# Fifty no-ops in ScalarE's stream, ahead of the skip products of the third tile

## The chip, the cores and the metric

The kernel runs on one core of one Trainium2 chip. The experiments came in three sets, each on another chip of this kind. The metric is the device time of one execution in microseconds (us). Before the change it was 213.41 us (median of 3 runs, 212.93 to 216.17). TensorE, VectorE, ScalarE, GpSimd and SyncE are called PE, DVE, ACT, POOL and SP in the profile; PEld is PE's weight load.

## The reference

It mixes a state-space branch and a dense branch over 2048 rows of width 640. Cut to what matters:

```python
def reference(A_x, ..., gate_w):
    x = A_x                                            # [1, 2048, 640]
    g = sigmoid((x * gate_w).sum(-1, keepdims=True))
    a = ssm(x)                                         # scan over the rows; ends in
                                                       #   y = 2*real(h @ C.T) + x * Dskip
    b = gelu(x @ w1 + b1) @ w2 + b2                    # 640 -> 1728 -> 640
    return g * a + (1 - g) * b
```

`x * Dskip` is the skip product of the title.

## The kernel before

The 2048 rows are four tiles of 512. The kernel lists its operations with their dependencies and assumed durations; a small scheduler in it fixes each engine's order, and waits are inserted for the dependencies. PE results go through eight PSUM banks, handed out in turn. One tile's output is made as follows (cuts marked with `...`):

```python
def outsT(q, mid=None):
    pieces = [(4, 0, HT), (4, HT, 512)] + [(d, 0, 512) for d in range(4)]
    mb = [next_bank() for _ in pieces]          # six banks for the second dense layer
    ...                                         # PE: mt_{q}, ScalarE evicts it to E1T (6 pieces)
            op(f"e1t_{q}_{d}_{t0}", "act", ..., [("bank", bank), ...], [("E1T", d, t0)], f_ev, prio=5)
    ...
    for d in range(KD):                         # KD = 5: the skip products, in place in xT

        def f_dx(d=d):
            return inc("act", nc.scalar.activation(xT[q][:, d, :], xT[q][:, d, :], ACT.Copy, scale=cols2[:, 1, d:d + 1]))

        op(f"dx_{q}_{d}", "act", d_act(512), [("cols2", 1)], XK0[d] if q == 0 else [("xT", q, d)], f_dx, prio=20)

    for d in range(KD):                         # five C-projection groups of ten matmuls
        bank = next_bank()                      # the third of them gets mb[0] again
        ...                                     # PE: ct_{q}_{d}; ScalarE evicts it to E2T
    ...
    op(f"s{q}", "dve", ..., K2, XT[q], lambda: tt(xf, xf, e2, ALU.add), prio=P)   # first reader of the products
```

The order on ScalarE is not that of the text. The third tile's products (q = 2) can run as soon as that tile's first-layer matmuls have read xT, so the scheduler puts them between that tile's Gelus and the E1T evictions of the second tile (q = 1).

Of the kernel before, what the change touches and what calls it, by code (L numbers as in the profile page):

```python
# [147 lines left out]
class Prog:  # L148
# [8 lines left out]
    def op(self, name, eng, dur, reads, writes, fn, prio=None, lat=0.0, after=()):  # L157
        deps = {}
        for k in reads:
            for w in self.last_w.get(k, ()):  # L160
                deps[w.idx] = w
        for k in writes:
            for w in self.last_w.get(k, ()):
                deps[w.idx] = w
            for r in self.last_r.get(k, ()):
                deps[r.idx] = r
        for a in after:
            deps[a.idx] = a
        deps = list(deps.values())
        E = self.E  # L170

        def run(eg, deps=deps, eng=eng, fn=fn):
            E.wait(eng, *[d.done for d in deps if not (eng == "pe" and d.eng == "pe")])
            return fn()

        it = self.sch.add(name, eng, dur, deps, run, prio=prio, lat=lat)
        for k in writes:
            self.last_w[k] = [it]
            self.last_r[k] = []
        for k in reads:  # L180
            self.last_r.setdefault(k, []).append(it)
        return it


def bass_gated_mix__ssm_conv_s5__dense_activation_gelu__prompt_kernel(
# [18 lines left out]
    _, S, D = A_x.shape  # L204
# [5 lines left out]
    NQ = S // 512  # L210
# [15 lines left out]
    with ExitStack() as es:  # L226
# [83 lines left out]
        def inc(eng, ins):  # L310
            return E.inc(eng, ins, eng + "_s")
# [8 lines left out]
        def d_act(n):  # L320
            return 0.26 + n * 0.00084
# [590 lines left out]
        def outsT(q, mid=None):  # L912
# [39 lines left out]
            for d in range(KD):  # L952

                def f_dx(d=d):
                    return inc("act", nc.scalar.activation(xT[q][:, d, :], xT[q][:, d, :], ACT.Copy, scale=cols2[:, 1, d:d + 1]))

                op(f"dx_{q}_{d}", "act", d_act(512), [("cols2", 1)], XK0[d] if q == 0 else [("xT", q, d)], f_dx, prio=20)
# [125 lines left out]
```

## Time and profile before

| | before |
|---|---|
| time, median (range) | 213.41 us (212.93 to 216.17) |
| profiled execution | 213.5 us, clock 1.00 |
| span of its instructions | 212.2 us |
| ScalarE idle between the third tile's products and the next eviction | 10.97 us |

The page of the profile, kernel before: busy time by engine with the share of the span, then the engines' shares of the chain of work that ended last.

```profile
PE 208.4 (98%) x1102; PEld 104.4 (49%) x1102; DVE 190.1 (90%) x240; ACT 103.2 (49%) x177; POOL 4.2 (2%) x12
...
PE 94%; SPq 2%; DMA 2%; issue 0%; DVE 0%
```

PE is the bound, and ScalarE is not in the chain at all. Next the ScalarE timeline around the third tile's products. The columns are start, duration, engine and line, operation, output <- input, count, and in brackets the idle time before with what ended it.

```profile
106.76 0.69 ACT L660 ACTIVATE Gl<-ps,cols 128x512 bf16<-128x512 f32 x1 [0.39 <-PE ps L653]
107.84 0.69 ACT L660 ACTIVATE Gl<-ps,cols 128x512 bf16<-128x512 f32 x1 [0.39 <-PE ps L653]
108.43 3.16 ACT L955 ACTIVATE xT<-xT,cols 128x512 bf16<-128x512 bf16 x5
122.56 3.15 ACT L938 ACTIVATE E1T<-ps,cols 128x256 bf16<-128x256 f32 x6 [10.97 <-PE ps L931]
```

The five products (L955) follow the last Gelu (L660) directly. Then ScalarE idles for 10.97 us until PE gives it something to evict. The PE timeline of the same stretch, kernel before:

```profile
107.64 14.22 PE L920 MATMUL ps<-Gl,W2sb 128*128 128x256 bf16 x78
121.80 0.71 PE L931 MATMUL ps<-Gt,W2sb 64*128 64x512 bf16 x6
122.44 10.96 PE L967 MATMUL ps<-Hb,CT 128*128 128x512 bf16 x50
```

There is no idle time in brackets: PE goes straight on. L967 is the C projection, five groups of ten matmuls. Its third group starts two fifths in, at about 122.5 + 2 x 2.16 = 126.8 us, and needs the bank that the first E1T eviction frees.

### The profile page before, as it was taken

The numbers are of one execution on the slowest core, as the hardware profiler recorded it, in microseconds if no ns is written. First come the engines' busy times: TensorE is split into PE (matmuls) and PEld (weight loads), VectorE is DVE, ScalarE is ACT, GpSimd is POOL, SyncE is SP. The second block draws the span as 40 slices with busy tenths as digits, with TensorE's granted clock in tenths as the row PEclk, the third lists the DMA queues.
The fourth block names the chain that finished last, engine by engine and source line by source line (L and its number), as shares of the span: only waits on it lengthen the run. The fifth ranks groups of instructions, "written<-read, shape, count | busy, mean of one in ns | idle before, by whom it ended". The sixth has DMA issues, their size and how long they took to land.

```text
span 212.2 us, 2742 instructions
## 1 busy us (share of the span) xinstructions
PE 208.4 (98%) x1102; PEld 104.4 (49%) x1102; DVE 190.1 (90%) x240; ACT 103.2 (49%) x177; POOL 4.2 (2%) x12
## 2 busy tenths in 40 slices
PE   8999999999999999999999999999999999999995
PEld 4344444444554444444464444444456444567774
DVE  2599999999999998999999999899999999499734
ACT  2579556679850453556680072456660037523320
POOL 1000000300000000000100000000010000000000
PEclk9999999999999999999999999999999999999999
DMA  6999999999300020063274000009440000007341
GB/s 170 279 238 192 176 209 298 277 173 225 76 0 3 5 44 0 0 127 76 48 62 111 3 0 0 0 2 166 95 124 39 0 3 0 0 0 109 87 116 63
DMA packets 48424, 19.08 MB, mean 90 GB/s; under 512 B 41372, under 2 KB 47132, under 8 KB 48412
## 3 DMA queue, kind: packets, MB, share of 16 engines
q1 hardware_dynamic: 46752, 17.59, 40.1%
q0 software_dynamic: 1600, 1.32, 4.3%
q8 instruction: 8, 0.13, 0.3%
q10 hardware_dynamic: 60, 0.01, 0.1%
q14 instruction: 4, 0.03, 0.1%
HBM read 8.41 MB, written 2.63 MB: 52 GB/s over the span
## 4 chain that ended last, share of the span: by engine, by line
PE 94%; SPq 2%; DMA 2%; issue 0%; DVE 0%
PE ps L653 22%; PE ps L696 20%; PE ps L920 20%; PE ps L967 15%; PE ps L783 7%; PE ps L832 5%; DMA W1sb<-in_B_w_dram 2%; PE ps L631 2%; SPq L340 1%; PE ps L674 1%; SPq L333 1%; PE ps L931 1%; PE ps L797 0%; DVE W1sb L866 0%
## 5 line engine op out<-in xcount | busy, mean ns | idle before, releaser
L653 PE MATMUL ps<-xT,W1sb 128*128 128x512 bf16 x220 | 48.1, 379 | 0.0
L736 DVE TENSOR_TENSOR_SCAN W<-atab,V 128x1280 bf16<-128x1280 f32 x16 | 44.3, 2811 | 0.3
L696 PE MATMUL ps<-xT,BT 128*128 128x512 bf16 x200 | 43.8, 379 | 0.0
L920 PE MATMUL ps<-Gl,W2sb 128*128 128x512 bf16 (+1 forms) x234 | 42.7, 344 | 0.0
L660 ACT ACTIVATE Gl<-ps,cols 128x512 bf16<-128x512 f32 x44 | 29.8, 693 | 15.5 <-PE ps L653 15.5
L653 PEld LDWEIGHTS ps<-xT,W1sb 128*128 128x128 bf16 x220 | 21.5, 98 | 26.0
L967 PE MATMUL ps<-Hb,CT 128*128 128x512 bf16 x150 | 32.9, 379 | 0.0
L920 PEld LDWEIGHTS ps<-Gl,W2sb 128*128 128x128 bf16 x234 | 22.9, 98 | 19.3
L705 ACT ACTIVATE U<-ps 128x512 bf16<-128x512 f32 x40 | 23.7, 596 | 15.6 <-PE ps L696 15.6
L696 PEld LDWEIGHTS ps<-xT,BT 128*128 128x128 bf16 x200 | 19.5, 98 | 23.7 <-ACT Gt L682 0.4
L938 ACT ACTIVATE E1T<-ps,cols 128x512 bf16<-128x512 f32 (+1 forms) x18 | 9.4, 624 | 36.0 <-PE ps L931 36.0
L967 PEld LDWEIGHTS ps<-Hb,CT 128*128 128x128 bf16 x150 | 14.5, 98 | 17.9 <-DVE V L488 0.6
L975 ACT ACTIVATE E2T<-ps 128x512 bf16<-128x512 f32 x15 | 9.1, 604 | 13.6 <-PE ps L967 13.6
L783 PE MATMUL ps<-W2sb,Gl 128*128 128x320 bf16 x104 | 14.8, 299 | 0.0
L606 DVE SCALAR_TENSOR_TENSOR trf<-xn,gwb 128x640 bf16<-128x640 bf16 x16 | 13.2, 822 | 0.4
L488 DVE TENSOR_TENSOR V<-V,W 128x1280 bf16<-128x1280 bf16 x16 | 12.5, 821 | 0.3
L488 DVE TENSOR_TENSOR Hb<-Hb,V 128x1280 bf16<-128x1280 bf16 x16 | 12.5, 821 | 0.3
L488 DVE TENSOR_TENSOR V<-mr,U 128x2560 bf16<-128x2560 bf16 x8 | 11.9, 1492 | 0.3
L783 PEld LDWEIGHTS ps<-W2sb,Gl 128*128 128x128 bf16 x104 | 10.1, 98 | 4.3 <-issue 0.3
L488 DVE TENSOR_TENSOR Hb<-c,W 128x2560 bf16<-128x2560 bf16 x8 | 11.9, 1489 | 0.2
L488 DVE TENSOR_TENSOR V<-s,W 128x2560 bf16<-128x2560 bf16 x8 | 11.9, 1484 | 0.0
L488 DVE TENSOR_TENSOR W<-mi,U 128x2560 bf16<-128x2560 bf16 x8 | 11.9, 1483 | 0.0
(91 smaller groups left out, 150.1 us busy)
## 6 DMA issues: line engine op xcount, KB each, us to landing
W2sb<-in_B_w_dram SPq DMA_DIRECT2D x1, 2080.0 KB, 8.6
out_dram<-xn SPq DMA_DIRECT2D x3, 640.0 KB, 4.8
W1sb<-in_B_w_dram SPq DMA_DIRECT2D x5, 256.0 KB, 4.1
xn<-in_A_x_dram POOLq DMA_DIRECT2D x2, 640.0 KB, 7.1
trf<-grow SPq DMA_DIRECT2D x3, 256.0 KB, 5.0
xn<-in_A_x_dram SPq DMA_DIRECT2D x1, 640.0 KB, 7.2
W1sb<-in_B_w_dram SPq DMA_DIRECT2D x1, 480.0 KB, 5.4
out_dram<-W1sb SPq DMA_DIRECT2D x3, 160.0 KB, 1.8
```

The source lines that it names most:

```text
L488: return inc("dve", nc.vector.tensor_tensor(out=o, in0=a, in1=b, op=o_))
L606: t = inc("dve", nc.vector.scalar_tensor_tensor(out=scr[:, :], in0=xn[q % 2][:, c, :], scalar=1.0, in1=gwb[:, :], op0=ALU.mult, op1=ALU.mu ...
L653: t = nc.tensor.matmul(PS[bank][:, :], W1sb[:, k, jf * 128:(jf + 1) * 128], xT[q][:, k, :], start=(k == 0), stop=(k == KD - 1))
L660: return inc("act", nc.scalar.activation(Gl[q % 2][:, jf, :], PS[bank][:, :], ACT.Gelu_apprx_tanh, bias=b1col[:, jf:jf + 1]))
L696: t = nc.tensor.matmul(PS[bank][:, :], BT[:, ci, kd, k * 128:(k + 1) * 128], xT[q][:, kd, :], start=(kd == 0), stop=(kd == KD - 1))
L705: return inc("act", nc.scalar.activation(dst, src, ACT.Copy, scale=1.0 if ci == 0 else -1.0))
L736: t = inc("dve", nc.vector.tensor_tensor_scan(out=g[:, ci, :], data0=a, data1=v[:, ci, :], initial=0.0, op0=ALU.mult, op1=ALU.add))
L783: t = nc.tensor.matmul(PS[bank][:, 0:HALF], Gl[q % 2][:, jf, t4 * 128:(t4 + 1) * 128], W2sb[:, jf, cols], start=False, stop=False, skip_gr ...
L832: t = nc.tensor.matmul(PS[bank][:, 0:n], H[b % NHB][:, ci, k, s * 128:(s + 1) * 128], CT[:, ci, k, cols], start=(i == 0), stop=(i == 2 * K ...
L920: t = nc.tensor.matmul(PS[bank][:, 0:t1 - t0], W2sb[:, jf, d * 128:(d + 1) * 128], Gl[q % 2][:, jf, t0:t1], start=(jf == 0), stop=False)
L938: return inc("act", nc.scalar.activation(E1T[:, d, t0:t1], PS[bank][:, 0:t1 - t0], ACT.Identity, bias=cols2[:, 0, d:d + 1]))
L967: t = nc.tensor.matmul(PS[bank][:, :].rearrange("p (s t) -> p s t", s=2), CT[:, ci, k, d * 128:(d + 1) * 128], Hb[:, 2 * (q % 2):2 * (q % ...
```

## The change

The intent is to see what fifty no-ops cost at a place where ScalarE has nothing to do afterwards. The whole diff:

```diff
@@ -952,6 +952,8 @@
             for d in range(KD):

                 def f_dx(d=d):
+                    for _ in range(10 if q == NQ - 2 else 0):
+                        nc.scalar.nop(nofuse=True)
                     return inc("act", nc.scalar.activation(xT[q][:, d, :], xT[q][:, d, :], ACT.Copy, scale=cols2[:, 1, d:d + 1]))
```

## The prediction

> **What bounds the kernel now.** TensorE. The busy-share table gives PE 208.4 us of a 212.2 us span (98%), VectorE 190.1 us (90%), ScalarE only 103.2 us (49%). The chain of work that ended last is 94% PE and holds no ScalarE instruction. ScalarE can cost time only where PE or VectorE waits for it.
>
> **What the change does.** Ten no-ops before each of the five ScalarE products that scale xT of tile q = 2 by the skip vector: 50 instructions, no data, no semaphore, nothing removed or moved. The durations that the kernel's scheduler uses are untouched: every engine keeps its order.
>
> **Where they fall.** In the ScalarE timeline the third tile's five products run from 108.43 to 111.59 us (about 0.71 us each, starts about 0.61 us apart), right after the tile's last Gelu (107.84 us). They cannot come earlier: they overwrite xT, which the first-layer matmuls read until 107.8 us. After them ScalarE sits idle for 10.97 us, until the matmuls for the next E1T eviction end at 122.5 us.
>
> **Cost of the no-ops.** The trace has no no-op on ScalarE; the closest is a bare semaphore instruction of its sequencer, recorded at 17 ns. [...] My estimate from these is 20 to 60 ns each, 1 to 3 us for 50. [...] ten no-ops (0.2 to 0.6 us) should hide under the product before them (0.61 us), and the first ten under the last Gelus. The products should end between 111.6 and 114.5 us.
>
> **Critical path.** None of it. Three slacks would have to be used up:
> 1. the 10.97 us before the E1T evictions: about 0.22 us per no-op, even if nothing overlaps;
> 2. then another 3.8 us or so: the first E1T eviction (over at 123.0 us) frees the bank that the third C-projection group takes at about 126.8 us;
> 3. the reader of the products, VectorE's first addition into this tile's xT, waits for E2T evictions that start at 176 us: over 60 us later.
>
> The stream grows by 3.2 KB (64 bytes an instruction); the trace shows a few 8 KB instruction reads of 0.4 to 0.7 us each. They may shift; that should not show.
>
> **Prediction.** 213.4 us, the time before. Range 212.6 to 214.8, the scatter of the runs (212.93 to 216.17 before). Faster by over 2%: 0.01. Within 2%: 0.97. Slower by over 2%: 0.02.
>
> **What would show it right or wrong.** The third set of products starts at 108.4 to 109.0 us, its starts 0.6 to 0.75 us apart; the idle time before the second set of E1T evictions shrinks from 10.97 us by 0 to 3 us; that set still starts at about 122.5 us, released by PE; PE's busy time stays about 208.4 us, with no hole between 107 and 134 us; the chain stays 94% PE.
>
> **What would make it wrong.** A no-op that costs over about 0.3 us[...], so that evictions come late and PE waits for banks; a stalled instruction fetch on ScalarE later, where the last tile's evictions have only about 1 us of idle each; or runs in a slower state.

The forecast's sum came to 213.4 us, the time before and nothing added: the 1 to 3 us for 50 no-ops were to fall into ScalarE's 10.97 us of idle time.

## The result

| | before | after |
|---|---|---|
| time, median (range) | 213.30 us (212.93 to 216.17, 4 runs) | 212.86 us (212.52 to 213.04, 4 runs) |
| span of the profiled execution | 212.2 us | 211.7 us |
| semaphore instructions on ScalarE | 6 | 7 |
| no-op records on ScalarE | 0 | 0 |

The ratio of after to before is 0.998 (95% interval 0.9961 to 0.9999). Ratios here are the mean time of one kernel's fast runs over the mean of the other's fast runs of the same rounds, so not quite the ratio of the medians beside them. All four runs of after and its profiled run are fast, at clock 1.00. Before's fourth run came with this result; its 216.17 us is just over 1.5% above its fastest run and so counts as slow, and its three fast runs have a median of 213.18 us.

The page of the profile, kernel after, busy time and chain. (A few matmul records are missing from this trace: 1088 of 1102.)

```profile
PE 208.0 (98%) x1088; PEld 104.8 (50%) x1102; DVE 190.2 (90%) x240; ACT 103.2 (49%) x177; POOL 4.2 (2%) x12
...
PE 97%; DMA 1%; issue 0%; DVE 0%
```

The ScalarE timeline, kernel after:

```profile
107.97 0.69 ACT L660 ACTIVATE Gl<-ps,cols 128x512 bf16<-128x512 f32 x1 [0.39 <-PE ps L653]
108.56 3.16 ACT L957 ACTIVATE xT<-xT,cols 128x512 bf16<-128x512 bf16 x5
122.68 3.15 ACT L938 ACTIVATE E1T<-ps,cols 128x256 bf16<-128x256 f32 x6 [10.97 <-PE ps L931]
```

The PE timeline, kernel after:

```profile
107.77 14.22 PE L920 MATMUL ps<-Gl,W2sb 128*128 128x256 bf16 x77
121.93 0.71 PE L931 MATMUL ps<-Gt,W2sb 64*128 64x512 bf16 x6
122.57 10.96 PE L969 MATMUL ps<-Hb,CT 128*128 128x512 bf16 x50
```

Everything in the middle is 0.13 us later (a start-up difference) and otherwise the same: 0.59 us from the last Gelu to the first product, five products in 3.16 us, 10.97 us idle. This is too good. Fifty instructions have left no record and moved nothing.

The compiled programs say why. ScalarE's stream has 191 instructions of 64 bytes before and 192 after (12,224 and 12,288 bytes), with not one no-op among them; the streams of the other four engines are the same byte for byte. A version with one plain no-op in place of fifty compiles to exactly the same instructions as the changed kernel. The plain no-ops are dropped on the way to the binary. Their one trace is this: a wait that used to ride on the first product (for the load of xT) became a semaphore instruction of its own, which the trace shows at 107.97 us, 17 ns long. So the prediction was made about fifty instructions, and the chip got one.

That leaves two questions. What would fifty real no-ops have cost? And is the 0.2% by which the changed kernel came out ahead scatter, or something?

For the second, compare the ends of the traces. VectorE's last addition and the issue of the last stores, kernel before:

```profile
209.09 0.91 DVE L866 SCALAR_TENSOR_TENSOR W1sb<-ps,gcol,W1sb 128x256 bf16<-128x256 f32 x2 [0.21 <-PE ps L832]
...
209.60 0.81 SPq L875 DMA_DIRECT2D out_dram<-W1sb  x2
```

The same, kernel after:

```profile
209.22 0.91 DVE L866 SCALAR_TENSOR_TENSOR W1sb<-ps,gcol,W1sb 128x256 bf16<-128x256 f32 x2 [0.21 <-PE ps L832]
...
209.73 0.81 SPq L875 DMA_DIRECT2D out_dram<-W1sb  x2
```

The work ends at 209.09 + 0.91 = 210.00 us before and at 210.13 us after, so after is even a little late. But the span ends 2.18 us later before (212.18) and 1.58 us later after (211.71). The span's end is SP's wait for the last store. "Tail" below is the time from VectorE's last end to the record of that wait: 2.15 us before, 1.56 us after. In the trace's DMA records, one 8 KB read of the instruction queue stands out: before, it comes 0.82 us after VectorE's last end, while the last store is landing; after, it comes 1.40 us ahead of it.

### The profile page after: what moved, and what is told of

Read it like the earlier page. It is cut to its first block, busy times and chain, and to the rows that moved or that the text cites. A ratio compares the mean times of both kernels' runs of the same rounds, so it can differ in the third digit from the quotient of the medians.

```text
span 211.7 us, 2729 instructions
## 1 busy us (share of the span) xinstructions
PE 208.0 (98%) x1088; PEld 104.8 (50%) x1102; DVE 190.2 (90%) x240; ACT 103.2 (49%) x177; POOL 4.2 (2%) x12
## 4 chain that ended last, share of the span: by engine, by line
PE 97%; DMA 1%; issue 0%; DVE 0%
PE ps L653 22%; PE ps L696 20%; PE ps L920 20%; PE ps L969 15%; PE ps L783 7%; PE ps L832 5%; PE ps L631 4%; DMA xn<-in_A_x_dram 1%; PE ps L674 1%; PE ps L931 1%; PE ps L419 1%; PE ps L797 0%; DVE W1sb L866 0%; PE ps L438 0%
## 5 line engine op out<-in xcount | busy, mean ns | idle before, releaser
L653 PE MATMUL ps<-xT,W1sb 128*128 128x512 bf16 x215 | 47.5, 379 | 0.3
L696 PE MATMUL ps<-xT,BT 128*128 128x512 bf16 x196 | 43.1, 379 | 0.3 <-issue 0.2
L783 PE MATMUL ps<-W2sb,Gl 128*128 128x320 bf16 x104 | 14.8, 299 | 0.0
```

Of the source, the lines that this page charges most:

```text
L653: t = nc.tensor.matmul(PS[bank][:, :], W1sb[:, k, jf * 128:(jf + 1) * 128], xT[q][:, k, :], start=(k == 0), stop=(k == KD - 1))
L696: t = nc.tensor.matmul(PS[bank][:, :], BT[:, ci, kd, k * 128:(k + 1) * 128], xT[q][:, kd, :], start=(kd == 0), stop=(kd == KD - 1))
L783: t = nc.tensor.matmul(PS[bank][:, 0:HALF], Gl[q % 2][:, jf, t4 * 128:(t4 + 1) * 128], W2sb[:, jf, cols], start=False, stop=False, skip_gr ...
```

## The experiments

"Kept" no-ops carry a one-letter text, `nc.scalar.nop(hint="n", nofuse=True)`; these stay in the program. No-ops with a cycle count also stay in it (fifty compile to 241 instructions on ScalarE), but the simulation that each kernel must pass first does not know them, so they could not be tried.

### Control, and the changed kernel again

`before_again` is the kernel before, with no edit.

> A control: the kernel before, submitted as if it were a new one. It measures how large a ratio plain scatter gives. If the 0.2% that the changed kernel came out ahead is scatter, this ratio should also stray from 1 by 0.1 to 0.3%, within 0.996 to 1.004. If it stays at 1.000 within 0.0005 while the changed kernel repeats 0.998, the 0.2% is real.

`as_given` is the changed kernel, with no edit.

> The changed kernel again, unchanged. In the compiled program no no-op is left: ScalarE's stream has 192 instructions of 64 bytes against 191 before, the one more being a semaphore instruction of 17 ns in the trace. Theory A (the no-ops were never executed, so nothing changed but one 17 ns instruction off the critical path): ratio 0.997 to 1.003, and again 7 semaphore instructions on ScalarE and no no-op record. Theory B (the no-ops are executed but invisible): same time, so this run alone cannot tell them apart; the kept no-ops of the next run can.

Measured: before_again 213.49 us against 213.47 us, ratio 0.9986 (0.9953 to 1.0019); as_given 212.88 us against the same 213.47 us, ratio 0.9979 (0.9937 to 1.0021). As_given again has 7 semaphore instructions on ScalarE and no no-op record. So plain scatter gives a ratio 0.14% off by itself, and the times alone cannot settle a gain of 0.2%. The tails can be compared: 2.36 us in before_again and 1.55 us in as_given, each like its own kind.

### Fifty no-ops that are really there

```diff
-                        nc.scalar.nop(nofuse=True)
+                        nc.scalar.nop(hint="n", nofuse=True)
```

> The same 50 no-ops, each with a one-letter text, which keeps them in the compiled program (241 plus 1 = 242 ScalarE... counted: 241 instructions, 50 of them no-ops). Theory A (the given no-ops were dropped): here, for the first time, no-op records appear on ScalarE between 107.9 and 114.5 us, 20 to 60 ns each, and the third tile's products get further apart or the group of five ends later by 0 to 3 us; the time stays within 0.5% because 10.97 us of ScalarE idle time follow (212.4 to 214.0 us). Theory B (the given ones were executed but not recorded): no no-op records here either, and the ScalarE timeline equals that of the changed kernel.

(The compiled stream has 241 instructions, 50 of them no-ops.) Measured: 213.07 us against 213.47 us, ratio 0.9968 (0.9937 to 0.9999), no cost. The trace now has 50 no-op records on ScalarE, each 14 ns long and mostly 39 ns after the one before; the first starts at 108.15 us and the last at 110.22 us. That is 2.07 us for 50. Theory A holds: the given ones were not there. ScalarE timeline of named50:

```profile
108.14 0.69 ACT L660 ACTIVATE Gl<-ps,cols 128x512 bf16<-128x512 f32 x1 [0.39 <-PE ps L653]
108.73 3.16 ACT L957 ACTIVATE xT<-xT,cols 128x512 bf16<-128x512 bf16 x5
122.86 3.15 ACT L938 ACTIVATE E1T<-ps,cols 128x256 bf16<-128x256 f32 x6 [10.97 <-PE ps L931]
```

Still 0.59 us from Gelu to product, 3.16 us for the five, 10.97 us idle. The no-ops of a group run while the engine is busy with the instruction before, so they delay not even ScalarE itself. This trace shows it: the last no-op belongs to the fifth product and started at 110.22 us, while the third product (from 109.95 us) was still running.

### How much room there is: real copies in place of no-ops

```diff
+        junk = SB("junk", [128, 512], BF16)
...
-                    for _ in range(10 if q == NQ - 2 else 0):
-                        nc.scalar.nop(nofuse=True)
+                    for i in range(4 if q == NQ - 2 else 0):       # 4, 5 or 6
+                        E.wait("act", inc("act", nc.scalar.activation(junk[:, :], xT[q][:, d, :], ACT.Copy)))
```

> Instead of no-ops, 4 real copies (128x512 into a spare tile) before each of the five products, each waiting for the one before it: I estimate 0.65 to 0.75 us each, so ScalarE is occupied 13 to 15 us longer. My slack sum of the prediction (10.97 us of idle, then about 3.8 us until PE needs the first freed bank, 14.8 us in all): cost 0 to 0.3 us. Rival (only the 10.97 us of ScalarE idle is free, everything above it reaches PE): 2 to 4 us. The result in xT must be right in both.

Measured: 212.98 us against 213.47 us, ratio 0.9968 (0.9931 to 1.0004). The ScalarE timeline of copies20, from the last group of copies to the first evictions:

```profile
121.56 2.60 ACT L957 ACTIVATE junk<-xT 128x512 bf16<-128x512 bf16 x4
124.19 0.72 ACT L958 ACTIVATE xT<-xT,cols 128x512 bf16<-128x512 bf16 x1
124.82 3.13 ACT L939 ACTIVATE E1T<-ps,cols 128x256 bf16<-128x256 f32 x6
```

(Each copy waits for the one before it: both write the same spare tile, a race otherwise.) A copy takes 0.65 us, so 13.1 us were added. The evictions start without any idle time before them, 2.2 us later than PE had them ready, and PE does not notice: its fifty C-projection matmuls run in one piece.

```profile
122.54 10.96 PE L970 MATMUL ps<-Hb,CT 128*128 128x512 bf16 x50
```

The idle time of ScalarE is therefore not the whole of the slack; the free banks add to it. The rival's 2 to 4 us are refuted.

Next come five copies and then six. Six were run first.

> 5 real copies before each product: 25 at 0.653 us, 16.3 us. copies30 cost 6.8 us where the slack sum gave 4.8 to 5.2: PE's wait was 4.92 us as summed, and the granted clock then read 0.50 for about 4 us after it. Theory C (the missing 2 us is the clock, which falls only after a long enough wait): here the first E1T eviction is over at about 128.6 us, PE waits 1.6 to 1.9 us from 126.9 us, the granted clock stays 1.00, and the time is 214.3 to 215.3 us. Rival (every wait for a bank brings a further cost of the same kind, in proportion or fixed): 2.3 us or more, with a clock under 1.00.

Measured: 214.80 us against 213.38 us, ratio 1.0048 (1.0001 to 1.0096), clock 1.00 in all four runs. The PE timeline of copies25:

```profile
122.04 4.49 PE L970 MATMUL ps<-Hb,CT 128*128 128x512 bf16 x20
128.13 6.65 PE L970 MATMUL ps<-Hb,CT 128*128 128x512 bf16 x30 [1.60 <-ACT E1T L939]
```

The wait is exactly where the sum put it, ahead of the third of the five groups, and released by the E1T eviction. It is 1.60 us long, with the clock at 1.00, so theory C holds. (This kernel's profiled execution also has the shorter tail, see below: 1.60 - 0.6 is about 1 us, and the ratio gives 1.0 us; the medians are 1.4 us apart.)

> 6 real copies before each product. copies20 showed 0.653 us a copy, so 19.6 us are added. My slack sum (14.8 us): PE stalls at the third C-projection group of the second tile (needed at about 126.9 us, first E1T eviction done at about 131.9 us), 4.8 to 5.2 us, so 217.4 to 218.4 us. Rival (only ScalarE's idle 10.97 us is free): 8.6 us, about 221.5 us. Second rival (a later stage gives the delay back, because VectorE or ScalarE catches up): less than 3 us.

Measured: 220.29 us against 212.96 us, ratio 1.0321 (1.0285 to 1.0358). The PE timeline of copies30:

```profile
122.51 4.49 PE L970 MATMUL ps<-Hb,CT 128*128 128x512 bf16 x20
131.92 9.11 PE L970 MATMUL ps<-Hb,CT 128*128 128x512 bf16 x30 [4.92 <-ACT E1T L939]
```

PE waits 4.92 us, as summed. But the cost is about 6.8 us (3.21% of 213 us), outside the range that I gave. The difference is in the matmuls after the wait: thirty of them take 9.11 us here and 6.65 us in copies25. The windows of copies30 show why (columns: stretch, length, busy us and instructions of PE, PEld, DVE, ACT, POOL, then the granted clock, DMA share and GB/s):

```profile
122.50:127.00 4.50, 4.50 (x22) 1.88 (x20) 4.43 (x7) 4.31 (x8) 0.00 (x0) 1.00 0.00 0
127.00:131.90 4.90, 0.00 (x1) 0.00 (x0) 4.76 (x9) 4.71 (x9) 0.00 (x0) 0.82 0.00 0
131.90:136.00 4.10, 4.08 (x10) 1.50 (x11) 1.39 (x2) 3.62 (x7) 0.00 (x0) 0.50 0.00 0
136.00:138.00 2.00, 2.00 (x8) 0.79 (x7) 0.24 (x2) 0.69 (x2) 0.00 (x0) 0.77 0.00 0
138.00:141.00 3.00, 3.00 (x16) 1.37 (x14) 0.00 (x0) 0.60 (x1) 0.00 (x0) 1.00 0.08 1
```

The granted clock (third number from the end) fell to half during the wait and stayed there until about 136.9 us (a mean of 0.77 from 136 to 138 us is 0.9 us at half and the rest at full); the trace's clock records have it at half from 130.1 to 136.9 us. The sum is then 4.92 us of wait, 9.11 - 6.65 = 2.46 us of half clock, less 0.6 us for the tail: 6.8 us. That it agrees so closely is partly chance: two of the four runs show a mean clock of 0.984 like the profiled one, the other two 0.992, so about half the loss. In the profiled executions waits of 1.60 us (copies25) and 2.41 us (next run) kept the clock at 1.00 and the one of 4.92 us did not. There the half clock began 3.1 us after PE's last matmul (127.0 to 130.1 us) and lasted for about 5 us of work (131.9 to 136.9 us). These runs do not show how long a wait has to be for it.

### How many no-ops it takes

```diff
-                    for _ in range(10 if q == NQ - 2 else 0):
-                        nc.scalar.nop(nofuse=True)
+                    for _ in range(96 if q == NQ - 2 else 0):
+                        nc.scalar.nop(hint="n", nofuse=True)
```

> 96 kept no-ops before each product, 480 in all. named50 took 2.08 us from the first no-op to the last, 41.6 ns each, so 480 take 20.0 us from 108.1 to 128.1 us; the last product then starts at about 128.1 us, and the first E1T eviction is over at about 129.2 us. Slack model: PE waits 2.0 to 2.8 us from 126.9 us, clock 1.00, time 215.0 to 216.3 us. Rival (a no-op never holds up ScalarE): no wait, 212.5 to 213.7 us. Second rival (the sequencer cannot fetch so many instructions that fast): spacing well over 42 ns at each page of 128 no-ops, and a larger cost.

Measured: 216.48 us against 213.38 us over all four runs, 215.39 us over the three fast ones; ratio 1.0125 (1.0033 to 1.0218). The verdict on the time is unclear at the 2% mark, so the profile decides. The profiled execution took 215.39 us, within the expected 215.0 to 216.3. The no-ops ran from 107.73 to 128.04 us. ScalarE and then PE in named480:

```profile
124.00 0.72 ACT L957 ACTIVATE xT<-xT,cols 128x512 bf16<-128x512 bf16 x1 [3.35 <-issue]
128.09 0.72 ACT L957 ACTIVATE xT<-xT,cols 128x512 bf16<-128x512 bf16 x1 [3.37 <-issue]
128.72 3.13 ACT L938 ACTIVATE E1T<-ps,cols 128x256 bf16<-128x256 f32 x6
```

```profile
122.33 4.49 PE L969 MATMUL ps<-Hb,CT 128*128 128x512 bf16 x20
129.23 6.65 PE L969 MATMUL ps<-Hb,CT 128*128 128x512 bf16 x30 [2.41 <-ACT E1T L938]
```

With 96 no-ops to a product there is far too little to hide under (96 at 39 ns are 3.7 us, a product takes 0.72 us), and ScalarE idles 3.07 to 3.65 us before each of the five products, for "issue" in this view. PE waits 2.41 us at the place of the slack model (2.0 to 2.8 expected). Two of the four runs were longer, 217.57 and 219.35 us (the latter counted as slow); both have a mean granted clock of 0.992 against 1.000 in the other two. The clock fell in them, but a mean of 0.992 over 217 us is only about 1.7 us lost (my estimate), and they are 2.2 and 4.0 us longer than the other two. Those runs have no trace, so why the clock fell and where the rest went stays open.

The second rival was partly right: at four places, 126 or 127 no-ops and one or two products from each other, two successive no-ops are 0.32 to 0.33 us apart where 0.039 us is usual. Together these are 128 instructions of 64 bytes, one 8 KB page. The pauses add 1.1 us in all, within the 20.3 us that the burst took. (A fifth gap, of 0.37 us at 109.9 us, lies at no such distance and is not explained.)

### The other engine: no-ops in PE's stream

```diff
                 def f_mm(d=d, bank=bank):                  # the C-projection groups; from the kernel before
+                    for _ in range(10 if q == 1 else 0):
+                        nc.tensor.nop(hint="n", nofuse=True)
                     t = None
```

> The same 50 kept no-ops in the stream of the engine that bounds the kernel: ten before each of the five C-projection groups of the second tile in TensorE's stream (groups of ten matmuls, 2.16 us each, from 122.5 us). Theory R (TensorE's sequencer too reads far enough ahead of its array): no hole in PE and 212.5 to 213.7 us. Rival (the sequencer of the busy engine has no lead, and each no-op costs what one costs on ScalarE, or the 51 ns that TensorE's semaphore instructions show): 2.0 to 3.0 us more, holes of 0.4 to 0.6 us before each group.

Measured: 213.32 us against 213.38 us, ratio 1.0009 (0.9932 to 1.0085). The interval is wide, so the profile decides. (It caught the longest of the four runs, 216.1 us: all of this stretch is 2.4 us later than in the kernel before.) PE timeline of pe50:

```profile
124.20 0.71 PE L931 MATMUL ps<-Gt,W2sb 64*128 64x512 bf16 x6
124.85 10.96 PE L969 MATMUL ps<-Hb,CT 128*128 128x512 bf16 x50
135.65 1.67 PE L696 MATMUL ps<-xT,BT 128*128 128x512 bf16 x7
```

The five groups take 10.96 us, the same as before, with no hole. The first no-op ran at 121.65 us, 3.2 us ahead of the group it stands before. Within a group the no-ops are mostly 70 to 71 ns apart here, more than on ScalarE. Even in the stream of the engine that bounds the kernel, ten no-ops in a row (about 0.7 us) hide here under the matmuls ahead of them.

### The tail: where the page boundary falls

```diff
# one_early
+                    if q == 0 and d == 0:
+                        nc.scalar.nop(hint="n", nofuse=True)
# named128, named129, named256 (n = 128, 129, 256)
+                    for _ in range(n if q == NQ - 2 and d == 0 else 0):
+                        nc.scalar.nop(hint="n", nofuse=True)
```

> One kept no-op, not in the third tile but before the first product of the first tile (at about 49 us). New theory P (page): what the change really altered is the length of ScalarE's stream, 192 instructions for 191, so that the 8 KB instruction read that came at 210.8 us in the kernel before, 0.8 us after VectorE's last instruction and while the last store was landing, comes before that instruction instead; the tail from VectorE's last end to the end of the span falls from 2.15 to 1.56 us. P expects here: the read before VectorE's last end (about 1.4 us before it), a tail of 1.50 to 1.65 us, ratio 0.9965 to 0.9990. Rival S (scatter, or something about the place in the third tile): a tail of 2.1 to 2.4 us as in both profiles of the kernel before, ratio 0.999 to 1.001.

> 128 kept no-ops, all before the third tile's first product. 128 instructions of 64 bytes are exactly 8 KB, one page, so theory P expects the boundary to fall again where it fell in the kernel before: an instruction read 0.5 to 1.3 us after VectorE's last end, a tail of 2.0 to 2.4 us, ratio 0.999 to 1.001. Rival S: as all the other changed kernels, tail 1.5 to 1.65 us. Both expect the no-ops themselves (128 at 39 ns, 5.0 us) to cost PE nothing.

> One no-op more than the run before. Theory P: the read is again ahead of VectorE's last end (1.2 to 1.6 us before it), a tail of 1.50 to 1.65 us, 0.4 to 0.8 us faster in the median than named128. Rival S: equal to named128 within 0.2 us.

> 256 kept no-ops before the third tile's first product, two whole pages of 128. Theory P: as in the kernel before and in named128, an instruction read after VectorE's last end (0.5 to 1.3 us) and a tail of 2.0 to 2.4 us. Rival (named128 was chance): a tail of 1.50 to 1.65 us. PE does not wait in either (256 at 41.6 ns are 10.7 us, under the 14.8 us of slack).

What the traces of all kernels show, by the number of instructions that ScalarE's stream has over the 191 of the kernel before. The read is the last 8 KB instruction read that moves with the length of ScalarE's stream (so I take it for ScalarE's; the 16 KB instruction reads, eight in before and eight in after, are on another queue), in us from VectorE's last end (negative: ahead of it).

| kernel | instructions more | the read | tail, us |
|---|---|---|---|
| before | 0 | +0.82 | 2.15 |
| before_again | 0 | +1.20 | 2.36 |
| pe50 (change on PE only) | 0 | +1.18 | 2.34 |
| named128 | 128 | +0.83 | 2.06 |
| named256 | 256 | +0.84 | 2.00 |
| after | 1 | -1.40 | 1.56 |
| as_given | 1 | -1.50 | 1.55 |
| one_early | 1 | -1.56 | 1.55 |
| named129 | 129 | -1.56 | 1.56 |
| copies20, 25, 30 | 20, 25, 30 | over 31 ahead | 1.55 to 1.56 |
| named50 | 50 | over 79 ahead | 1.56 |
| named480 | 480 | over 84 ahead | 1.55 |

Theory P's tails came true in all four runs made to test it, and no kernel breaks the pattern. A stream longer by a whole number of pages has the read in the tail and loses 0.45 to 0.8 us there; one instruction more, at whatever place, and it does not. The sharpest pair is 128 against 129.

The pattern holds in each of the three sets of runs, so the chip is not the reason: before_again against as_given, named128 against named129, pe50 and named256 against copies25.

The times are much less clear than the tails, because starts differ by over 2 us from run to run (as_given's profiled run reached the third tile's products 2.2 us late, having waited for its first loads). One_early came out at 213.31 us against 212.96 us, ratio 0.9995 (0.9971 to 1.0020); named128 is 213.53 us, ratio 1.0030 (0.9988 to 1.0071). Both miss the ranges that I gave P. Named129 is 213.12 us, ratio 1.0009 (0.9970 to 1.0048); named256 is 213.24 us, ratio 0.9977 (0.9908 to 1.0046). Named129 is 0.41 us faster than named128 in the median, the lower edge of what P expected, with ranges that overlap.

Put together by set, the fast runs of the kernels in which PE does not wait say this. In the first set the median is 213.48 us with the read in the tail (before and before_again, 17 runs) and 212.98 us without (as_given, named50, copies20; 16 runs). In the second set it is 213.16 us with (before and named128, 17 runs) and 213.26 us without (one_early, named129; 12 runs). The third set has no such kernel without the read. (Before was not profiled again in the second and third sets; I place it by its stream.) The gain of the first set did not come back in the second. So the shorter tail is shown in the profiled executions, and a gain in the median is not shown: the 0.2% by which the changed kernel came out ahead stays open.

That the read causes the later landing is shown by moving it by one instruction (named128 and named129: from 0.83 us after to 1.56 us ahead, tail 2.06 and 1.56 us). The packet records of the same traces show how. The last store ends with 16 completion marks. Fifteen of them come within 1.55 us of VectorE's last end in every kernel. The sixteenth comes at 1.53 to 1.54 us without the read and at 1.98 to 2.34 us with it. And in all five traces with the read, a sixteenth of the last store's packets (eight of 256 bytes and one of 4) starts just as the read ends, in the order of the table:

| | before | before_again | pe50 | named128 | named256 |
|---|---|---|---|---|---|
| the read ends, us after VectorE's last end | 1.41 | 1.51 | 1.49 | 1.38 | 1.35 |
| those nine packets start | 1.40 | 1.50 | 1.48 | 1.38 | 1.35 |

Without the read all packets are over by 1.20 us. So a share of the last store starts only when the instruction read has ended. That both are on one DMA engine is not shown, since the records do not name it; and why the last mark then takes 0.5 to 0.7 us from the last packet, where 0.35 us is usual, is open.

## Why the prediction was right or wrong

**The time: right.** 213.4 us were predicted with a range of 212.6 to 214.8; 212.86 us were measured, within 2% of before. This alone is no evidence for the mechanism, since the fifty instructions were not there; named50, in which they were, took 213.07 us and is the evidence.

**"Ten no-ops before each of the five ScalarE products ... 50 instructions": wrong, and the step that failed.** The program on the chip contains none of them. ScalarE's stream grew by one semaphore instruction of 17 ns. The prediction took the source for the program, and the time could not tell it, because the slack covers both. Only the missing records and the unchanged 0.59 us, 3.16 us and 10.97 us gave it away.

**The cost of a no-op, "20 to 60 ns each, 1 to 3 us for 50": right for real ones.** The record is 14 ns, the spacing 39 ns, 50 take 2.07 us. What stands behind the estimate is the 17 ns record of a semaphore instruction, and the measured spacing is over twice as much. The upper end of the range, not its source, took it in.

**"Should hide under the product before them": right.** This was an assumption when it was written. Named50 leaves the products' starts 0.61 us apart, with ten no-ops 39 ns apart before each.

**The slacks: right, and the first two tested to their end.** The sum of 10.97 and about 3.8 us is 14.8 us; 13.1 us of added work cost nothing, 16.3 us made PE wait 1.60 us (1.5 by the sum), 19.6 us made it wait 4.92 us (4.8 by the sum). What the sum left out is that the wait of 4.92 us also cost clock: another 2.46 us in copies30. The third slack of the prediction, up to the reader of the products, was never reached.

**"About 0.3 us" per no-op as the threshold: not tested as such.** It is the slack sum, 14.8 us over 50, and a real no-op costs 39 ns. Reached by number instead, 480 no-ops made PE wait 2.41 us, as the same sum gives.

**"They may shift; that should not show": wrong in a small way.** The instruction reads did shift, and it shows as 0.6 us in the tail of the profiled execution. The prediction looked for a stalled ScalarE; it was the last store that had been late, in the kernel before.

**"The chain stays 94% PE": not kept, but not by the change.** It reads 97% in after and 98% in before_again, which has no edit; what differs is the first 14 us.

**No stall later on ScalarE:** none seen. A page boundary inside a burst of no-ops cost 0.32 to 0.33 us in named480, but with no-ops alone.

## What to carry to other kernels

Before you cost an instruction, make sure that it is in the compiled program: count the instructions of the engine's stream, and ask a trace for its record; an edit that moves nothing at all has perhaps not been made. The slack of an engine off the critical path was here its idle time plus the time until the bound engine needs the first buffer that it frees (10.97 and 3.8 us), and once that was used up the cost was more than the wait where TensorE's clock fell in it (after 4.92 us of wait, not after 1.60 or 2.41 us). The length of an instruction stream moved the end of the profiled executions by 0.45 to 0.8 us here, so give a one-instruction change a control of the same length before you explain a gain of a few tenths of a percent, and compare runs of the same set.
